# One wait of a load queue is moved from normalised rows to a weight transfer

## The chip, the cores and the metric

The kernel runs on one core of a Trainium2 chip. The core has five engines with a queue of instructions each: TensorE (PE in the profile; its weight loads are listed as PEld), VectorE (DVE), ScalarE (ACT), GpSimd (POOL) and SyncE (SP), which here only issues transfers. Transfers are issued from SP, from POOL and, at the start, from ACT, and all of them are carried by the same 16 DMA engines. The metric is the device time in microseconds of one execution, as a median of several runs.

## The reference

Two blocks follow each other. The first is cosine attention over 8 batches of 12 heads, 448 rows of 64 elements each:

```python
q_n = q / (norm(q) + 1e-6);  k_n = k / (norm(k) + 1e-6)
scores = q_n @ k_n.T / tau            # tau = 0.1
attn = softmax(scores)
attn_out = attn @ v
x = attn_out.transpose(0, 2, 1, 3).reshape(3584, 768)
```

The second is a two-layer product with a leaky ReLU between:

```python
h = x @ w_in                          # 768 -> 2048
g = maximum(0.01 * h, h)
out = g @ w_out                       # 2048 -> 768, float32
```

All inputs are float32. The kernel computes its products in bf16 with float32 sums.

## The kernel before, in words

**Slots.** Queries and keys are handled in 48 slots. In the first two batches (slots 0 to 11, six for each batch) a slot is one pair of heads, with its q and its k. From slot 12 on, two pairs of heads form a unit, and each unit has two slots, or halves: the even slot is the q half, the odd slot the k half. The third batch begins there: slot 12 is the q half of the first unit, slot 13 its k half, slot 14 the q half of the second unit and slot 15 its k half.

**The way of a slot.** `load_qk` (lines 142 to 165) issues its transfers from SP into one of four rotating buffers (`qk_h`); from slot 12 on, these are two transfers of 64 partitions, both on line 150. `squares` multiplies the rows by themselves on POOL (line 216 from slot 12 on, line 224 before). `sums` adds them up on VectorE (line 232; line 238 before slot 12). `roots` takes the norms on ScalarE (lines 245 and 246). `normalise` divides on VectorE (lines 253, 254, and 260 or 270), which writes `qn` and, with the squares, sets the buffer free for the slot four further on. `transposes` then turns the tile: through TensorE (line 284) for early slots, through VectorE (line 306) and six SP transfers per unit (line 315) from slot 12 on.

**What uses it.** `scores` forms the products of q and k on TensorE (line 346) and their exponentials on ScalarE (line 355). `attend` forms the row totals and the products with v on TensorE (line 366), inverts the totals on ScalarE (lines 377 and 378) and scales on VectorE (line 397). The units use lines 417, 423, 442 and 467 or 473 for the same.

**The two-layer product.** `first` (line 494) multiplies with `w_in_sb` and puts the result through the leaky ReLU on ScalarE (line 505); `second` (line 531) multiplies with `w_out_sb`, and VectorE copies the result out of PSUM (line 541) for SP to store (line 548). For the first chunk of rows `second` takes all its tiles against the first half of the output columns, and then all against the second half. `feed_groups` puts such groups into the stream of TensorE between the steps of attention.

**Weights.** `load_w_in` and `load_w_out` issue from POOL and convert from float32 to bf16 on the way. `load_w_out(1)`, the second half of the output columns, is called on line 777, and its last column is the last column of `w_out_sb`. POOL also issues the loads of v (lines 176, 184 and 202).

**Order.** All instructions stand in an order written out by hand; every engine takes its own in that order, and one that waits holds all behind it. Eight PSUM banks are dealt out by `banks` (line 75), which hands out the one used longest ago. Two helpers hold a queue back on purpose:

```python
def hold_loads(s):
    nc.sync.dma_start(out=behind, in_=qn[s][0:1, 6, 0, 0:1])

def hold(x):
    gp.tensor_copy(out=seen, in_=x)
```

`hold_loads(s)` is a transfer of a single element out of the normalised rows of slot s. Its data is not used: SP cannot issue it, nor what stands behind it, before `qn[s]` is written. `hold` does the same to POOL.

In the stretch of the change, s is 6, so that `load_qk(s + 6)` loads slot 12, and so on. The SP queue reads: hold on slot 9, load 12, hold on slot 10, load 13, hold on slot 11, load 14, load 15 (line 832), load 16 (line 842). On POOL, the squares of slots 12 and 13 follow the `hold` of slot 11 (`settle`, line 805), and those of slot 14 follow the `hold` of slot 12. On VectorE, `sums(13)` (line 834) stands ahead of the copies of the output tiles fed after it; on ScalarE, `roots(13)` (line 836) stands ahead of the exponentials of line 838.

Of the kernel before, what the change touches and what calls it, by code (L numbers as in the profile page):

```python
# [16 lines left out]
def kernel(  # L17
# [10 lines left out]
    nc = tc.nc  # L28
    B, H, S, D = q.shape
    N_tok, D_model = out.shape  # L30
# [10 lines left out]
    MT = D_ff // 128  # L41
# [56 lines left out]
    w_out_sb = cpool.tile([128, MT, D_model], BF16, name="w_out_sb")  # L98
# [43 lines left out]
    def load_qk(s):  # L142
        if s >= NSLOT:
            return
        whole = ldp.tile([128, 14 * D], F32, name="qk_h")
        if s >= OLD:
            u, which = divmod(s - OLD, 2)
            for w, pair in enumerate(UNITS[u][1]):
                b, h0 = pair // NPAIR, 2 * (pair % NPAIR)
                nc.sync.dma_start(  # L150
                    out=whole[64 * w : 64 * w + 64],
                    in_=(q, k)[which][b, h0 : h0 + 2].rearrange("h (p t) d -> (h p) (t d)", t=14),
                )
            raw[s] = whole
            return
        b, h0 = s // NPAIR, 2 * (s % NPAIR)
        q_h, k_h = halves(whole)
        nc.sync.dma_start(out=q_h[:, :, 0:3], in_=main(q, b, h0, 2))
        nc.sync.dma_start(out=k_h, in_=main(k, b, h0, 2))
        for i, x in enumerate((q, k)):  # L160
            nc.sync.dma_start(
                out=q_h[64 * i : 64 * i + 64, :, 3],
                in_=x[b, h0 : h0 + 2, MAIN:S].rearrange("h p d -> p h d"),
            )
        raw[s] = (q_h, k_h)
# [5 lines left out]
    def load_v(j):  # L171
        if j >= B * NQ:
            return
        b, jj = divmod(j, NQ)
        vb[j] = vbp.tile([128, 4, 3, D], BF16, name="v_b")
        gp.dma_start(out=vb[j], in_=main(v, b, 4 * jj, 4))
# [405 lines left out]
    behind = cpool.tile([1, 1], BF16, name="behind")  # L582
# [29 lines left out]
    def hold_loads(s):  # L612
        nc.sync.dma_start(out=behind, in_=qn[s][0:1, 6, 0, 0:1])
# [133 lines left out]
    s, j = NPAIR, NQ - 1  # L747
# [46 lines left out]
    hold(qn[s + 4][:, 6, 0, 0:1])  # L794
    squares(s + 5)
    load_v(s // 2 + 2)
    hold_loads(s + 4)
    load_qk(s + 7)
    feed_groups(0, 1)

# [4 lines left out]
    def settle(s, more=()):  # L805
        normalise(s)
        if s >= OLD:
            transposes(s)
        hold(qn[s][:, 6, 0, 0:1])
        for x in (*more, s + 2):  # L810
            squares(x)
# [7 lines left out]

    scores(s + 3, (0, 1, 2))  # L820
    settle(s + 5, (s + 6,))
    hold_loads(s + 5)
    load_qk(s + 8)
    feed_groups(0, 1)
    sums(s + 6)
# [66 lines left out]
    for n, tiles in enumerate(visits):  # L892
        s = preps.get(n, NSLOT)
# [98 lines left out]
```

## Time and profile before

| what | us |
|---|---|
| median of 3 runs (416.55 to 417.8) | 416.8 |
| the profiled execution's own time | 416.43 |
| its span, first to last instruction | 414.6 |
| TensorE busy | 407.1 |
| ScalarE busy | 250.2 |
| VectorE busy | 221.5 |
| POOL busy | 114.6 |
| `w_out_sb`, issue to landing, 2 transfers (least and most) | 21.3, 23.2 |
| `qk_h` from the k input, from slot 12 on, issue to landing (median) | 4.3 |

Times within the span count from its first instruction. An engine is counted as busy only in its own arithmetic; the issue of a transfer is not counted. In the timeline a row gives start, length, engine, line, operation, what is written and read, the number of like instructions merged into the row, and in brackets how long the engine had stood idle and what released it. The queue of transfers issued by POOL is q0, that of those issued by SP and ACT is mainly q1; the DMA view gives packets, MB and the time that the packets took as a share of 16 engines, which can pass 100% since packets overlap.

### The profile page before, as it was taken

What the parts mean: (1) busy time and instruction counts of PE and PEld (TensorE: products, weight loads), DVE (VectorE), ACT (ScalarE), POOL (GpSimd) and SP (SyncE); (2) the same over time, 40 slices, a digit from 0 to 9 for tenths busy, and PEclk for the clock granted to TensorE, in tenths of its full rate; (3) what the DMA queues carried; (4) which work ended last, traced back from release to release, by engine and by line L of the source; (5) the groups of instructions that cost most, each with busy time, mean ns of one, the idle gap of its engine ahead of it and who ended that gap; (6) DMA issues with size and microseconds to landing.
All of it is one profiled execution on the core that took longest, in us unless ns stands there. A gap on an engine that the chain in (4) does not pass through costs nothing.

```text
span 414.6 us, 11342 instructions
## 1 busy us (share of the span) xinstructions
PE 407.1 (98%) x4799; PEld 212.3 (51%) x4799; DVE 221.5 (53%) x387; ACT 250.2 (60%) x431; POOL 114.6 (28%) x149
## 2 busy tenths in 40 slices
PE   8899999999999999999999999999999999999997
PEld 3335555544555555544455555554445555654565
DVE  6977976855778556766474964464621301210022
ACT  5997876378657785668865688547764464004300
POOL 4875543433234132413331433122210000000000
PEclk9999999999999999999999999999999999999999
DMA  7999998775377851884275681742442100020022
GB/s 195 242 214 220 210 234 187 181 223 129 60 206 182 204 132 22 204 229 99 53 186 157 151 229 43 175 126 84 91 90 68 51 39 3 38 77 0 2 76 76
DMA packets 41964, 53.82 MB, mean 130 GB/s; under 512 B 12474, under 2 KB 32314, under 8 KB 41914
## 3 DMA queue, kind: packets, MB, share of 16 engines
q1 hardware_dynamic: 25738, 41.01, 35.0%
q0 software_dynamic: 15488, 11.80, 19.7%
q8 instruction: 37, 0.61, 0.6%
q10 hardware_dynamic: 688, 0.30, 0.2%
q14 instruction: 13, 0.11, 0.1%
HBM read 45.61 MB, written 11.01 MB: 137 GB/s over the span
## 4 chain that ended last, share of the span: by engine, by line
PE 87%; DMA 4%; ACT 3%; DVE 3%; POOL 2%; SPq 1%; issue 1%; POOLq 0%
PE ps L531 34%; PE ps L494 34%; PE ps L442 9%; PE ps L417 7%; ACT pe L355 2%; DMA qk_h<-in_k_dram 2%; PE ps L366 2%; DVE qn L270 1%; DMA xT<-in_k_dram 1%; DMA xT<-in_q_dram 1%; POOL sq L224 1%; PE ps L346 1%; POOL sq L216 1%; DVE ss L238 0%; SPq L131 0%
## 5 line engine op out<-in xcount | busy, mean ns | idle before, releaser
L531 PE MATMUL ps<-w_out_sb,hT 128*128 128x384 bf16 (+1 forms) x912 | 151.3, 324 | 0.3 <-DVE xT L397 0.3
L494 PE MATMUL ps<-xT,w_in_sb 128*128 128x384 bf16 (+1 forms) x768 | 151.1, 353 | 0.0
L423 ACT ACTIVATE pe<-ps 128x896 bf16<-128x896 f32 x126 | 108.9, 915 | 46.1 <-PE ps L417 46.1
L531 PEld LDWEIGHTS <-hT 128*128 128x128 bf16 x912 | 86.5, 98 | 64.3 <-issue 10.0
L494 PEld LDWEIGHTS <-w_in_sb 128*128 128x128 bf16 x768 | 72.6, 98 | 74.3 <-issue 9.7
L505 ACT ACTIVATE hT<-ps 128x384 bf16<-128x384 f32 (+1 forms) x128 | 67.4, 552 | 56.0 <-PE ps L494 55.0
L541 DVE COPY osb<-ps 128x384 f32<-128x384 f32 (+1 forms) x57 | 31.2, 548 | 100.7 <-PE ps L531 100.6
L216 POOL TENSOR_TENSOR sq<-qk_h 128x896 f32<-128x896 f32 x36 | 61.0, 1695 | 9.2 <-DMA qk_h<-in_k_dram 7.7
L616 POOL CAST seen<-qn 128x1 f32<-128x1 bf16 x46 | 8.5, 185 | 169.4 <-DVE qn L260 160.5
L260 DVE TENSOR_TENSOR qn<-qk_h,r 128x896 bf16<-128x896 f32 x36 | 42.4, 1176 | 1.2
L232 DVE TENSOR_REDUCE ss<-sq 128x14 f32<-128x910 f32 x36 | 38.0, 1054 | 1.1 <-POOL sq L216 1.1
L355 ACT ACTIVATE pe<-ps 128x896 bf16<-128x896 f32 x42 | 35.9, 917 | 1.8 <-PE ps L346 1.7
L417 PE MATMUL ps<-qkT 64*32 64x448 bf16 x1008 | 36.5, 353 | 0.0
L253 DVE TENSOR_REDUCE r<-norms 128x14 f32<-128x28 f32 x48 | 8.6, 178 | 48.3 <-ACT norms L246 47.7
L467 DVE TENSOR_TENSOR xT<-ps,rb 128x448 bf16<-128x448 f32 x32 | 18.4, 617 | 23.2 <-PE ps L442 21.5
L306 DVE STREAM_TRANSPOSE tt<-qn 128x448 f32<-128x448 f32 x36 | 29.6, 821 | 0.9
L442 PE MATMUL ps<-pe,vq 64*32 64x448 bf16 x1008 | 27.0, 349 | 0.0
L245 ACT ACTIVATE ss<-ss 128x14 f32<-128x14 f32 x48 | 10.3, 214 | 25.4 <-DVE ss L232 24.4
L417 PEld LDWEIGHTS <-qkT 64*32 64x32 bf16 x1008 | 13.1, 91 | 19.2 <-issue 14.5
L442 PEld LDWEIGHTS <-vq 64*32 64x32 bf16 x1008 | 14.5, 92 | 8.0 <-issue 0.3
L442 PE MATMUL ps<-pe,ones 64*32 64x448 bf16 x560 | 15.1, 349 | 0.0
L346 PE MATMUL ps<-qkT 64*64 64x448 bf16 (+1 forms) x132 | 12.9, 359 | 2.1 <-ACT pe L355 1.2
(53 smaller groups left out, 218.9 us busy)
## 6 DMA issues: line engine op xcount, KB each, us to landing
qk_h<-in_q_dram SPq DMA_DIRECT2D x36, 224.0 KB, 4.0
qk_h<-in_k_dram SPq DMA_DIRECT2D x36, 224.0 KB, 4.3
out_dram<-osb SPq DMA_DIRECT2D x20, 384.0 KB, 2.3
qkT<-tt SPq DMA_DIRECT2D x72, 56.0 KB, 3.3
qkT<-tt SPq DMA_DIRECT2D x36, 112.0 KB, 3.5
vq<-in_v_dram POOLq DMA_DIRECT2D x16, 224.0 KB, 5.0
w_in_sb<-in_moe_w_in_dram POOLq DMA_DIRECT2D x4, 768.0 KB, 11.2
w_out_sb<-in_moe_w_out_dram POOLq DMA_DIRECT2D x2, 1536.0 KB, 22.3
```

The source lines that it names most:

```text
L216: gp.tensor_tensor(sq[:, :, :D], x, x, op=ALU.mult)
L232: nc.vector.tensor_reduce(ss[s], sqs[s], axis=AX.X, op=ALU.add)
L260: nc.vector.tensor_tensor(qn[s].rearrange("p m d e -> p m e d"), raw[s].rearrange(f"p ({t[1:-1]} d) -> p m e d", e=n, d=D), r.rearrange(f" ...
L306: nc.vector.transpose(out=to.rearrange(("p g (c m) -> p m g c", "p g (m c) -> p m g c")[which], m=7), in_=qn[s].bitcast(F32).rearrange("p ...
L355: nc.scalar.activation(out=dst, in_=sc[:, :, :S], func=AF.Exp, scale=inv_tau)
L417: nc.tensor.matmul(out=sc[32 * strip : 32 * strip + 32, a, :S], lhsT=x[rows, c0 : c0 + 32], rhs=x[rows, 0:S], start=True, stop=True,)
L423: nc.scalar.activation(out=pq[u, i], in_=sc[:, :, :S], func=AF.Exp, scale=inv_tau)
L442: nc.tensor.matmul(out=po[32 * strip : 32 * strip + 32, w, :S], lhsT=weights, rhs=pq[us[x if two else 0], i][rows, a, :], start=(i == 0), ...
L494: nc.tensor.matmul(out=pm[:, :n], lhsT=w_in_sb[:, kt, m * 128 : (m + 1) * 128], rhs=xT[c // 2][:, kt, c0 : c0 + n], start=(done + i == 0), ...
L505: nc.scalar.activation(out=hT[c][:, m, :n], in_=pm[:, :n], func=AF.Prelu, alpha=0.01)
L531: nc.tensor.matmul(out=po2[:, : hi - lo], lhsT=hT[c][:, m, ts * 128 : (ts + 1) * 128], rhs=w_out_sb[:, m, half * HALF + lo : half * HALF + ...
L541: nc.vector.tensor_copy(out=o[:, cols], in_=po2[:, : hi - lo])
```

## The change

The one-element transfer ahead of load 13 reads the last element of `w_out_sb` in place of an element of `qn[10]`, so that SP waits there until `load_w_out(1)` has landed. The one-element transfer ahead of load 14 is removed. Loads 13, 14 and 15 stand behind the new wait. Everything else keeps its order.

```diff
@@ -794,7 +794,7 @@
     hold(qn[s + 4][:, 6, 0, 0:1])
     squares(s + 5)
     load_v(s // 2 + 2)
-    hold_loads(s + 4)
+    nc.sync.dma_start(out=behind, in_=w_out_sb[0:1, MT - 1, D_model - 1 :])
     load_qk(s + 7)
     feed_groups(0, 1)
 
@@ -819,7 +819,6 @@
 
     scores(s + 3, (0, 1, 2))
     settle(s + 5, (s + 6,))
-    hold_loads(s + 5)
     load_qk(s + 8)
     feed_groups(0, 1)
     sums(s + 6)
```

## The prediction

> **What bounds the kernel now.** I read the first part of the page, then the list of waits of TensorE, then the chain of work between 40 and 95 us, and last the timeline and the DMA view of the stretch that the change touches. The page:
>
> ```profile
> PE 407.1 (98%) x4799; PEld 212.3 (51%) x4799; DVE 221.5 (53%) x387; ACT 250.2 (60%) x431; POOL 114.6 (28%) x149
> ```
>
> TensorE is busy for 98%, and from 60 us to the end its list of waits holds one entry of 0.3 us, at 70.49 us. So the order of work on TensorE after 60 us is a block without holes: whatever stops it there for a microsecond adds about a microsecond. The chain of work (start, length, what) says what TensorE leans on shortly before 70 us:
>
> ```profile
> 54.85 7.55 DMA qk_h<-in_k_dram
> ...
> 64.72 1.11 DVE ss L232
> ```
>
> This is load 13 (the k half of the first unit): it landed at 62.40, was squared on GpSimd (POOL) and summed on VectorE, and its root was taken on ScalarE at 65.86. The chain runs through this load already, so a later landing meets almost no reserve. Timeline, with idle time and releaser in brackets:
>
> ```profile
> 49.12 1.16 POOL L110 DMA_DIRECT2D w_out_sb<-in_moe_w_out_dram  x1
> ...
> 53.64 0.60 SPq L613 DMA_DIRECT2D behind<-qn  x1
> ...
> 54.33 1.11 SPq L150 DMA_DIRECT2D qk_h<-in_k_dram  x2
> ...
> 62.53 2.16 POOL L216 TENSOR_TENSOR sq<-qk_h 128x896 f32<-128x896 f32 x1 [3.64 <-DMA qk_h<-in_k_dram]
> ...
> 64.72 1.10 DVE L232 TENSOR_REDUCE ss<-sq 128x14 f32<-128x910 f32 x1 [0.51 <-POOL sq L216]
> ...
> 65.74 0.55 DVE L541 COPY osb<-ps 128x384 f32<-128x384 f32 x1
> ...
> 67.27 0.75 PE L366 MATMUL ps<-pe,ones 128*32 128x448 bf16 x12
> ...
> 70.49 4.99 PEld L531 LDWEIGHTS <-hT 128*128 128x128 bf16 x32 [0.69 <-DMA w_out_sb<-in_moe_w_out_dram]
> ```
>
> POOL stood 3.64 us for load 13. The second half of the output weights left at 49.12, took 21.3 us (the landing time of its tile's view), so it landed at 70.4, and TensorE's weight load stood for it until 70.49. Last, how fast the POOL queue (q0), on which these weights travel, moves when the other queue is quiet, from 56 to 58 us:
>
> ```profile
> q0 software_dynamic: 540, 0.41, 132.0%
> q1 hardware_dynamic: 4, 0.00, 0.3%
> ```
>
> 0.41 MB in 2 us, 0.205 MB/us, the weights' own pace.
>
> **The change part by part.** Edit 1: the one-element transfer in front of load 13 waits for the second half of the output weights instead of for the norms of slot 10. Before, SP was released at 53.6; now at T, when the weights land. The instruction list of the changed kernel has the semaphore of that POOL transfer at this place, where VectorE's stood. Edit 2: the transfer in front of load 14 goes. Load 14 then follows load 13 at once.
>
> T, step by step. The weights are 1536 KB, 98 kB for each of 16 engines; 0.205 MB/us over 16 is 12.8 kB/us, so 7.7 us. They queue behind a v load issued at 48.31 whose landing took 8.5 us: the slowest engine gets to the weights at 56.8. 56.8 + 7.7 = 64.5. A second way: from 58 to 71 us queue q1 held 49.7% of the engines, 6.5 us, most of it loads 13 to 16, which now wait; 70.4 - 6.5 = 63.9. Lower bound: all engines finish together; from 58 us on q0 moved 1.10 MB, of which 0.2 MB is the next v load, and 0.90 MB at 0.205 is 4.4 us: 62.4. Upper bound: nothing is gained from the quiet, 70.4. I take 64.5, since the landing is that of the slowest engine.
>
> From T to load 13's landing: the release at 53.64 and the start of its second half at 54.85 are 1.21 us apart; then the landing. In the stretch of 72 to 100 us, without weights under way, loads on this line took 3.4, 4.1 and 5.8 us (least, median, most). I take 4.1: T + 5.3, 69.8 instead of 62.4.
>
> Who stands behind it. POOL squares slot 13 (1.68 us, the median of its group), with slot 14 queued after it. VectorE's sum of slot 13 starts 0.14 + 1.70 after the landing, 71.6, and queued behind it on VectorE stands the copy at 65.74 that empties a PSUM bank; it ends 1.57 us after the sum's start, at 73.2. The next instruction of TensorE that needs this bank is the row of totals at 67.27 (by the rotation of the banks in the code: the bank of the second half-0 output tile is the next single one to be dealt). So TensorE stops at 67.3 and goes on at landing + 3.46 = T + 8.8 = 73.3: 6.0 us later. ScalarE's root of slot 13 (65.86) starts at 72.8, +6.9, and the three exponentials queued behind it too; TensorE needs the first at 68.04 + 6.0 and has it (67.07 + 6.9 = 74.0): no more added.
>
> What it gives back: the wait for the weights at 70.49 goes. TensorE itself stood 0.26 us: -0.26.
>
> What is late next: the turned tile of unit 0 (VectorE 72.57, then six transfers on SP from 73.37 to 77.14, landing 3.3 us later, 80.4) is needed by TensorE at 80.9. With +6.9 it lands at 87.3; TensorE would be there at 86.6, so up to 0.7 us more if nothing else slows TensorE.
>
> TensorE after a stop. Before shows no stop of over 1 us but the one at the start: after 1.65 us of idleness the 512-column products followed each other every 0.425 us for 5.1 us, and from 6.75 us on every 0.21:
>
> ```profile
> 5.89 0.15 PEld L605 LDWEIGHTS <-pe 128*128 128x128 bf16 x1 [0.28 <-issue]
> 6.32 0.15 PEld L605 LDWEIGHTS <-pe 128*128 128x128 bf16 x1 [0.28 <-issue]
> 6.75 1.44 PEld L605 LDWEIGHTS <-pe 128*128 128x128 bf16 x7 [0.28 <-issue]
> ```
>
> 12 products at 0.21 us too much are 2.5 us. After a stop of 6 us this can come back: 0 (it belongs to the start alone) to 2.5. I take 2.5, as the nearest row is that of a TensorE that has stood; it also covers the 0.7 us above. Beside it stands the Trainium skill, "TensorE: Matmul & The Clock Gate", Part 1: the array falls to half its clock after an idle window of about 3.4 us, and climbs back after a busy one. By that rule a 6.0 us stop is long enough and the sum is the one below; without it, it would be rival A's. No run here shows a stop of this length in the middle of the kernel.
>
> Costed at nothing: the transfer that is gone (0.6 us of SP, which stands from 64.4 to 73.4 anyway), and with it the completion semaphores of later transfers move by one, all of long-landed ones. Loads 14, 15 and 16 leave at T + 1.9 to T + 5.6 and land by 76 at the latest; their squares stood at 66.26, 72.81 and 76.67 and come at 71.6 (right behind slot 13's), 79.7 and 83.6: POOL's queue covers 15 and 16, and load 14, landed by about 72, is followed by a sum that comes only at 80. If that cover went, the sum of slot 14 would be next.
>
> Sum: 6.0 - 0.26 + 2.5 = +8.2 us. The profiled execution took 416.43 us: 424.6. It stands 0.37 us under the median of 416.8, inside the spread of the three runs.
>
> **The rivals.**
> A. The same stop without the slow restart: 6.0 - 0.26 + 0.7 = +6.4, 422.9. For it: no slow stretch after the start in before; against it: no stop in before to try it.
> B. The weights land at the lower bound, 62.4, and load 13 in 3.4 us: the stop is 62.4 + 1.21 + 3.4 + 3.46 - 67.27 = 3.2, so +2.9, 419.4; with the restart 421.9. For it: an emptier DMA. Against it: the slowest engine starts on the weights at 56.8.
> C. The weights gain little: T near 70.4. The stop is 70.4 + 8.8 - 67.3 = 11.9, and +14.1 with the restart, 430.6. For it: first to last engine now spread over some 7 us. Against it: 6.5 us of q1 traffic really goes.
> D. Not slower. The hold opens so early that load 13 lands no later than TensorE can bear. Its stop is T - 58.5; it vanishes for T up to 58.5, and then only the 0.26 us is gained: 416.2, no measurable change. For it: loads took up to 7.5 us while the weights were under way, and 4.1 after, so the later start buys 3.4 us. Against it: 1.57 MB in 9.4 us after issue, behind a v load that itself lands at 56.8; q0 never kept over 0.205 MB/us in the stretches I read. By the fit in the Trainium skill, "DMA: Bandwidth & Descriptors", Anatomy of one DMA (2.0 us + bytes / 436 GB/s), 1.57 MB would take an estimated 5.6 us and land at 54.7, so D would hold and the time be D's 416.2. The trace disagrees: 21.3 us for this transfer, and 11.2 us (median) for one of half its size.
>
> **How the numbers follow.** Chances: forecast (T of 63.5 to 66.5 with a restart cost) 0.50; A 0.17; B 0.12; C 0.14; D 0.07. The range leaves out the upper half of C, the lowest of B and D: 419.5 to 429.5. About 0.3% (1.25 us) is what a measurement of this kernel can tell from no change. A, B, C and the forecast are slower by more than that: 0.93. D is 'same' but for unknown gains from the emptier DMA: same 0.05, faster 0.02.
>
> **What would show it.** In the changed profile: the one-element transfer and load 13 leave SP near 64 to 65 us; POOL's squares on line 216 wait some 11 us for that load; VectorE's sum on line 232 starts near 71.6; TensorE has a hole of about 6 us before the totals on line 366, released by VectorE's copy; the weights' wait on line 531 is gone; products after the hole are spaced at twice their time for some microseconds, or the granted clock dips. It is wrong if the weights land before 60 us, if the hole is absent, or if TensorE finds other work in it (its order is fixed, so I see none).

## The result, and the profile after

The changed kernel took 424.02 us (median of 6 runs, 422.52 to 424.49) against 417.02 us of the kernel before (6 runs). The ratio is 1.0163, with a 95% interval of 1.0144 to 1.0181: 7.0 us slower. The forecast was 424.6, between 419.5 and 429.5, and slower. The profiled execution took 424.18 us, 7.75 more than that of before. Every ratio below is to runs of the kernel before that were made along with it.

The list of waits of TensorE from 50 us to the end (who waits and for whom; us in total, times, longest), in the changed kernel:

```profile
PE ps L366 <- DVE osb L541: 5.9, 1, 5.9
PE ps L494 <- issue: 0.2, 1, 0.2
```

Before, the same list had one entry (what it waited for is settled below, with the third experiment):

```profile
PE ps L531 <- DVE xT L397: 0.3, 1, 0.3
```

Now there is one stop of 5.9 us, at the totals on line 366, and it is VectorE's copy out of PSUM that ends it. The wait on line 531 is gone. The chain of work says what the copy was late for (start, length, what):

```profile
49.43 15.24 DMA w_out_sb<-in_moe_w_out_dram
...
64.70 0.60 SPq L797
...
65.91 4.28 DMA qk_h<-in_k_dram
...
70.33 1.69 POOL sq L216
...
72.04 1.10 DVE ss L232
73.14 0.48 DVE osb L541
73.62 0.04 issue
73.66 4.09 PE ps L366 x36
```

The chain goes back from TensorE over the copy, the sum, the squares and load 13 to the transfer of the output weights, which ends at 64.68. In the timeline of before, SP had been let go for load 13 at 53.64. Before, queue q1, on which the loads of q and k travel, had moved 0.45 MB between 58 and 61 us. Now, between 57 and 61 us, the DMA view shows no traffic of q1, and of the POOL queue q0 this (packets, MB, share of 16 engines):

```profile
q0 software_dynamic: 1051, 0.81, 130.6%
```

0.81 MB in 4 us is the 0.20 MB/us of before: the quiet lets the weights keep their own pace, and no more. They land after 15.2 us instead of 21.3. The timeline around the stop, with idle time and releaser in brackets:

```profile
65.02 2.77 PE L531 MATMUL ps<-w_out_sb,hT 128*128 128x384 bf16 x16
...
70.32 1.68 POOL L216 TENSOR_TENSOR sq<-qk_h 128x896 f32<-128x896 f32 x1 [10.98 <-DMA qk_h<-in_k_dram]
...
72.04 1.10 DVE L232 TENSOR_REDUCE ss<-sq 128x14 f32<-128x910 f32 x1 [7.38 <-POOL sq L216]
...
73.17 0.22 ACT L245 ACTIVATE ss<-ss 128x14 f32<-128x14 f32 x1 [9.28 <-DVE ss L232]
...
73.66 1.31 PE L366 MATMUL ps<-pe,ones 128*32 128x448 bf16 x12 [5.87 <-DVE osb L541]
```

POOL stands for 10.98 us, VectorE for 7.38, ScalarE for 9.28, and TensorE, the only one whose time counts, for 5.87. The 12 products of the totals then take 1.31 us; before, they took 0.75. Busy time by stretch (TensorE, its weight loads, VectorE, ScalarE, POOL, then granted clock, DMA share and GB/s) says why:

```profile
69.00:70.00 1.00, 0.00 (x0) 0.00 (x0) 0.00 (x0) 0.00 (x0) 0.00 (x0) 1.00 0.96 251
70.00:71.00 1.00, 0.00 (x0) 0.00 (x0) 0.00 (x0) 0.00 (x0) 0.68 (x1) 0.59 1.01 244
...
76.00:77.00 1.00, 1.00 (x19) 0.43 (x15) 0.00 (x0) 0.97 (x3) 0.00 (x0) 0.50 0.00 0
77.00:78.00 1.00, 1.00 (x24) 0.37 (x16) 0.83 (x2) 0.10 (x1) 0.00 (x0) 0.99 0.00 0
```

The granted clock falls to 0.50 near 70.2 (0.59 over that microsecond is 0.18 us of full clock), during the stop, and is back at 77.0. TensorE worked for 3.35 us of that time, from 73.66 on, at half rate.

The account: from the start of the totals to the first product against the second half of the weights, TensorE took 3.22 us before (67.27 to 70.49), of which it stood 0.26. After, it took 4.52 (73.66 to 78.18). So the restart, the loss by the half rate after the stop, cost 4.52 - 2.96 = 1.56 us. The totals would have followed the row of line 531 at 65.02 without a gap, near 67.72 (2.70 later, as 64.57 and 67.27 stood before): they came 5.94 late. 5.94 + 1.56 - 0.26 = 7.24. The row on line 531 moved by 7.69, of which 0.44 was there already at the products on line 346 (60.48 before, 60.92 after), ahead of the stop and not explained here. The span grew by 7.8.

### The profile page after: what moved, and what is told of

Its sections match the earlier page's. It is cut to its first block, busy times and chain, and to the rows that moved or that the text cites. A ratio compares the mean times of both kernels' runs of the same rounds, so it can differ in the third digit from the quotient of the medians.

```text
span 422.4 us, 11322 instructions
## 1 busy us (share of the span) xinstructions
PE 406.8 (96%) x4783; PEld 212.7 (50%) x4799; DVE 220.8 (52%) x387; ACT 250.6 (59%) x431; POOL 114.6 (27%) x149
## 4 chain that ended last, share of the span: by engine, by line
PE 83%; DMA 8%; DVE 3%; POOL 2%; ACT 2%; issue 1%; SPq 1%; POOLq 0%
PE ps L531 33%; PE ps L494 31%; PE ps L442 9%; PE ps L417 7%; DMA w_out_sb<-in_moe_w_out_dram 4%; DMA qk_h<-in_k_dram 3%; PE ps L366 2%; DVE qn L270 1%; POOL sq L224 1%; DVE ss L238 1%; ACT pe L355 1%; DMA xT<-in_q_dram 1%; POOL sq L216 0%; PE ps L346 0%; POOL v_rem L184 0%
## 5 line engine op out<-in xcount | busy, mean ns | idle before, releaser
L216 POOL TENSOR_TENSOR sq<-qk_h 128x896 f32<-128x896 f32 x36 | 60.5, 1681 | 15.2 <-DMA qk_h<-in_k_dram 15.1
L442 PE MATMUL ps<-pe,ones 64*32 64x448 bf16 x560 | 15.1, 349 | 0.0
```

Of the source, the lines that this page charges most:

```text
L216: gp.tensor_tensor(sq[:, :, :D], x, x, op=ALU.mult)
L442: nc.tensor.matmul(out=po[32 * strip : 32 * strip + 32, w, :S], lhsT=weights, rhs=pq[us[x if two else 0], i][rows, a, :], start=(i == 0), ...
```

## The experiments

Theory M: the cost is the late landing of load 13, passed on through POOL, VectorE and one PSUM bank to TensorE, and a slow restart. Its rivals were that the bunch of loads 14 to 16 costs (R), that waiting on the weights' tile costs by itself (W), that every microsecond of delay costs its share (L), and that the slow rows after the stop have nothing to do with the stop (C).

**The second edit alone.** Against the kernel before:

```diff
-    hold_loads(s + 5)
```

> Only the second edit: the hold ahead of load 14 is gone, the hold ahead of load 13 still waits for the norms of slot 10. Theory M (the cost is load 13's late landing, handed on through POOL, VectorE and one PSUM bank to TensorE): load 13 leaves SP at 54.3 as before; load 14 now leaves right behind it, some 3 us earlier, and may make load 13 and the weights land up to 1 us later: 416.8 to 418.2. Rival R (loads 14 to 16 crowding is what costs): 420 or more.

Measured: 416.88 us (10 runs), a ratio to the kernel before of 0.9987 (0.9975 to 0.9998), so 0.1% faster at most, near the edge of what can be told. Load 14 left SP at 55.97 instead of 58.97, and POOL took up the squares of slot 13 at 63.25 (62.53 before). R is wrong as far as this edit goes. In its profile the weights landed after 22.0 us instead of 21.3, and TensorE stood 0.87 us for them instead of 0.26; the median shows nothing of it.

**The first edit alone.** Against the kernel before:

```diff
-    hold_loads(s + 4)
+    nc.sync.dma_start(out=behind, in_=w_out_sb[0:1, MT - 1, D_model - 1 :])
```

> Only the first edit: load 13 waits for the weights, and the hold on slot 11 stays ahead of load 14. Slot 11 is normalised at 57 us, long before SP gets there, so the kept transfer costs SP only some 0.7 us. Theory M: as the changed kernel, 423.3 to 424.8, TensorE stopped about 5.9 us before the totals. Rival R (both edits are needed, since loads 14 to 16 in a bunch cost): clearly less, 418 to 421.

Measured: 423.71 us (4 runs), ratio 1.0154 (1.0134 to 1.0174), not apart from the changed kernel's 1.0163. Its waits of TensorE from 50 us on:

```profile
PE ps L366 <- DVE osb L541: 5.9, 1, 5.9
```

The same stop at the same place. The whole loss is in the first edit. The restart is not the same, though: from the start of the totals at 72.99 to the first product against the second half of the weights at 78.23 TensorE took 5.24 us, so that by the account above the restart cost 2.28 us here, against 1.56. The granted clock fell at 71.08 and was back at 77.91, so that TensorE worked for 4.92 us at half rate instead of 3.35.

**The same wait, one load later.** Against the kernel before:

```diff
-    hold_loads(s + 5)
+    nc.sync.dma_start(out=behind, in_=w_out_sb[0:1, MT - 1, D_model - 1 :])
```

> The wait for the weights stands one load later: load 13 keeps its hold on slot 10, load 14 waits for the weights in place of slot 11, and 15 and 16 stand behind it. Theory M: load 13 lands near 62 as before; the weights land near 66 to 67, load 14 near 72, just about when its squares are due (sum of slot 14 stood at 73.1): 416.6 to 418.0. Rival R (the bunch behind the weights is what costs, whichever load leads it): 421 to 424.

Measured: 417.21 us (10 runs), ratio 0.9993 (0.9978 to 1.0009): no difference. SP in its timeline:

```profile
53.95 1.11 SPq L150 DMA_DIRECT2D qk_h<-in_k_dram  x2
66.66 0.60 SPq L822 DMA_DIRECT2D behind<-w_out_sb  x1
67.35 1.11 SPq L150 DMA_DIRECT2D qk_h<-in_q_dram  x2
```

Load 13 leaves at 53.95 as in the kernel before, and loads 14 to 16 stand behind the weights until 66.66, later even than in the changed kernel. That costs nothing: TensorE has no stop at the totals, its wait for the weights is gone, and the sum of slot 14 comes at 74.0 (73.1 before), from which a wait of 0.6 us on line 417 remains. (The profile of before names VectorE's line 397 for the wait on line 531. Here that row begins at 70.10, while the first scaling on line 397 runs from 69.74 to 70.37, and it does not wait; so before it was the weights that it waited for.) So neither the bunch (R) nor the wait on this tile (W) is the price. It is which load stands first behind it.

**A wait on the same tile that ends early.** Against the changed kernel:

```diff
-    nc.sync.dma_start(out=behind, in_=w_out_sb[0:1, MT - 1, D_model - 1 :])
+    nc.sync.dma_start(out=behind, in_=w_out_sb[0:1, MT - 1, 0:1])
```

> The changed kernel with the waiting transfer reading an element of the first half of the weights, which landed at 52.3 in the profile of before, so the wait ends no later than the old one at 53.6. Theory M: load 13 leaves at 54 as before, 416.8 to 418.2, like the kernel that only drops the second hold. Rival W (waiting on the weights' tile costs by itself, by its semaphore or by what the queue does behind it): 421 to 424.

Measured: 417.14 us (10 runs), ratio 1.0001 (0.9987 to 1.0015). The waiting transfer left SP at 52.83 and load 13 at 53.52. Only the moment of the release matters; W is out.

**A smaller dose.** Against the changed kernel, the wait is on the v load that was issued just ahead of the weights:

```diff
-    nc.sync.dma_start(out=behind, in_=w_out_sb[0:1, MT - 1, D_model - 1 :])
+    nc.sync.dma_start(out=behind, in_=vb[s // 2 + 1][0:1, 3, 2, D - 1 :])
```

> A smaller dose: the changed kernel with the waiting transfer reading the last element of the v load issued at 48.3, which landed at 56.8, so the release comes some 3 us later than before instead of 11. Theory M (the stop is the landing of load 13 minus 63.8, and nothing before that): load 13 leaves at 57.5 and lands between 62.1 (4.1 us) and 65.6 (7.5 us, as the weights are still under way), so a stop of 0 to 1.8 us, too short for a slow restart: 416.8 to 418.8, with about 418 if the landing is slow. Rival L (each us of delay costs its share, no reserve): 3 of 11 us, so 419.

Measured: 419.07 us (6 runs), ratio 1.0039 (1.0027 to 1.0052), by the ratio 1.6 us slower than the kernel before: just above the range of M, on the number of L. The median alone does not tell them apart; the profile does. Load 13 in its chain of work:

```profile
57.26 0.60 SPq L797
...
58.47 6.70 DMA qk_h<-in_k_dram
```

and its waits of TensorE from 50 us on, with the row on line 417 from its timeline below them:

```profile
PE ps L366 <- DVE osb L541: 1.1, 1, 1.1
PE ps L417 <- DVE xT L397: 0.5, 2, 0.3
```

```profile
82.00 0.57 PE L417 MATMUL ps<-qkT 64*32 64x448 bf16 x16
82.87 0.35 PE L417 MATMUL ps<-qkT 64*32 64x448 bf16 x1 [0.30 <-DVE xT L397]
```

With the weights still under way the load needs 6.70 us and lands at 65.2. This profile runs 0.2 us late (60.69 at the products on line 346, 60.48 before), so the formula of the prediction gives 65.2 - 0.2 - 63.8 = 1.2 us, and the stop is 1.1. Load 13 lands 2.6 us later than before and the stop is 1.1, so some 1.5 us were reserve: L, which has none, is out. The rest is a second wait, 0.5 us, on line 417, which the expectation had left out. It is not for the turned tile of unit 0, which the prediction named as late next: the first 16 products of the row read that tile and do not wait. The next one writes to a bank that VectorE's scaling on line 397 still has to empty (82.19 to 82.82), and it starts 0.05 us after that, at 82.87. The scaling comes late because the sums and roots ahead of it in the queues of VectorE and ScalarE do. The clock stays at 1.00. 1.1 + 0.5 - 0.26 = 1.3 us, of the 1.6 measured.

**TensorE kept busy, first try.** Against the changed kernel, ahead of the totals:

```diff
+    for i in range(60):
+        nc.tensor.matmul(
+            out=ps[:, 0, S:512], lhsT=id128, rhs=id128[:, : 512 - S],
+            start=(i == 0), stop=(i == 59),
+        )
     attend(NQ + 1)
```

> The changed kernel with 60 small products of constants (128x128 weights, 64 columns) given to TensorE just before the totals, where it stands still; their output goes to unused columns of PSUM. Theory M: the stop stays, as its cause is elsewhere, the clock stays at 1.0, and the slow restart (about 1.7 us in the profile of the changed kernel) goes: 422.0 to 422.9, against 424.0. Rival C (the rows after the stop are slow for another reason, such as PSUM or the operands just written): 423.7 to 424.5. If the small products take longer than the stop, some tenths are added.

Measured: 428.42 us (5 runs), ratio 1.0257 (1.0234 to 1.0279). It does not test what it was for. The small products wrote to columns that nothing uses, but in a bank whose exponential was still to come, and its wait came with it:

```profile
74.93 3.15 PE L841 MATMUL ps<-id 128*128 128x64 bf16 x60 [8.02 <-ACT pe L355]
78.01 0.75 PE L366 MATMUL ps<-pe,ones 128*32 128x448 bf16 x12
```

The stop became longer, 8.0 us, and the products came after it. It shows that this bank was not free; whether another was is not shown. The granted clock fell here too, at 70.87, and was back at 77.70. The small products filled the rest of the slow time, and the totals behind them took 0.75 us again, after a stop of 8.0 us, which fits the clock as the cause of the slow rows.

**TensorE kept busy, in its own bank.** Against the changed kernel, the output tile just ahead of the stop is computed three times over, the last time for use:

```diff
-            for m in range(MT):
+            for m in (3 if (c, ts, half) == (0, 2, 0) else 1) * list(range(MT)):
```

> The changed kernel, in which the output tile of TensorE just ahead of the stop (16 products, 2.7 us) is computed three times over into its own bank, the last time for use: 32 products more, some 5.2 us, inside the 5.9 us in which TensorE stood. In the try before, the small products had stood behind the exponentials and so not filled the stop. Theory M (the stop costs 5.9 us and the halved clock after it 1.7): the totals start when they did, the clock stays at 1.0, 422.0 to 422.9 (424.0 less 1.7 and what the shorter second window takes). Rival C (the slow rows after the stop come from something else than the stop): 423.7 to 424.5, clock still 0.99.

Measured: 422.99 us (4 runs), ratio 1.0141 (1.0128 to 1.0155), between the two ranges and next to that of M. Its timeline and its stretches:

```profile
64.60 7.97 PE L531 MATMUL ps<-w_out_sb,hT 128*128 128x384 bf16 x48
72.51 0.75 PE L366 MATMUL ps<-pe,ones 128*32 128x448 bf16 x12
```

```profile
70.00:72.00 2.00, 2.00 (x14) 1.22 (x13) 1.11 (x2) 0.00 (x0) 0.98 (x2) 1.00 1.03 249
72.00:74.00 2.00, 2.00 (x36) 1.03 (x38) 1.01 (x2) 1.94 (x5) 1.58 (x1) 1.00 0.76 181
```

5.2 us of added work fill the stop, the granted clock stays at 1.00, and the totals take 0.75 us again instead of 1.31. C is out: it is the stop that makes the rows after it slow. The mean granted clock of all four timed runs is 0.999 or 1.000, and that of the six runs of the changed kernel 0.991 to 0.995. The gain against the changed kernel is 1.0 us by the medians, less than the 1.56 us of the restart; TensorE now waits 0.5 us on line 417, for the scaling on line 397 as in the smaller dose. The intervals of the two ratios overlap (1.0128 to 1.0155, 1.0144 to 1.0181), so the time alone does not show the gain; the clock and the rows do.

**Not from the change: the weights issued first.** Against the kernel before, from which the hold ahead of load 14 is taken out too (not shown in the lines below):

```diff
-    load_v(s // 2 + 1)
     load_w_out(1)
+    load_v(s // 2 + 1)
```

> Not from the change: the kernel before without the hold ahead of load 14, and the second half of the output weights issued from POOL ahead of the v load of line 176 instead of behind it. The weights then start on the engines one v load (0.2 MB, about 1 us) earlier and should land near 70, about when TensorE wants them (70.2); its wait for them (0.9 us in the kernel without the hold) shrinks: 416.2 to 417.0 against 417.0 to 417.4 for the kernel before. Rival: the v load, now last, is late for the products on line 366 at 67.9, and takes back as much or more: 417 to 418.

Measured: 421.23 us (6 runs), ratio 1.0079 (1.0059 to 1.0100): a clear miss. What the rival named came about, the late v load, but at more than its price of 417 to 418. The v load behind 1.5 MB of weights on the same queue landed after 22.0 us:

```profile
71.45 0.75 PE L366 MATMUL ps<-pe,v_b 128*32 128x448 bf16 x12 [3.39 <-DMA v_b<-in_v_dram]
```

TensorE stood for 3.39 us, and in the profiled run that was enough for the clock:

```profile
72.00:73.00 1.00, 1.00 (x23) 0.49 (x16) 0.49 (x1) 0.00 (x0) 0.00 (x0) 0.73 0.07 17
...
75.00:76.00 1.00, 1.00 (x6) 0.47 (x4) 0.96 (x2) 0.98 (x2) 0.00 (x0) 0.56 0.00 0
```

Not in every run: in two of the six the mean granted clock was 1.000, and they took 419.07 and 419.52 us; in the other four it was 0.992 to 0.996, and they took 421.16 to 421.85.

## Why the prediction was right

| step | forecast | measured |
|---|---|---|
| weights land, SP is let go (T) | 64.5 | 64.68 |
| second half of load 13 leaves, after T | 1.21 | 1.23 |
| its landing time | 4.1 | 4.28 |
| POOL's wait for it | 11 | 10.98 |
| sum of slot 13 begins | 71.6 | 72.04 |
| TensorE's stop | 6.0 | 5.9 |
| wait for the weights, gone | -0.26 | gone |
| slow restart | +2.5 | +1.56 |
| sum, profile against profile | +8.2 | +7.24, and 0.44 from ahead of the stretch |

The forecast, 424.6, is nearer to the measured 424.02 than its terms are to theirs: the restart was put 0.94 us too high, and 0.44 us that nobody forecast came in ahead of the stretch. The two moments in the table, T and the sum of slot 13, carry such a late start as well: the weights were issued at 49.43 instead of 49.12. That part of the agreement is luck; the path and the stop are not.

**T.** The longer of the two ways was right. From issue to landing the weights took 15.1 to 15.8 us in the four profiles in which load 13 stands behind them; the two ways gave 15.4 and 14.8. That fits the reason given, that the landing is that of the slowest engine, which first has to finish the v load ahead. That load landed after 8.6 us here (8.5 before), and the weights then kept 0.20 MB/us. That the stretch before the change showed this pace at all, in the 2 us in which the other queue was quiet, is what made T a sum of rows.

**The way of the delay.** Squares, sum, copy, bank, totals: all in the order forecast, each released by the one before it. The first edit alone brings the whole loss, the second none, and the same wait one load later costs nothing. A release that comes 3 us late instead of 11 gives the stop of the formula (1.1 us for 1.2), so the reserve in the formula, from 62.4 to 63.8, is also right. The prediction's sentence that a later landing meets "almost no reserve" does not fit its own formula: it is 1.4 us. Not run was the copy put ahead of the sum on VectorE, which would try that link alone; it rests on the rows of the profiles.

**The restart.** Here the size was off. The step took the 2.5 us of the start of the kernel, where TensorE worked at half rate for 5.1 us. In the middle of the kernel the half rate lasted longer, 6.8 us (70.2 to 77.0), but it began during the stop, and TensorE worked for only 3.35 us of it: 1.56 us lost. With the first edit alone it worked for 4.92 us of it and lost 2.28, close to the 2.5, behind a stop of the same 5.9 us. The term that holds is the working time inside the slow stretch, times a little under a half. That the start of the kernel was slow for the same reason, the clock, was a reading from the spacing of its products; it holds, as the trace of before records the rise of the clock at 6.84 us, where the spacing halves. (The windows view prints 1.00 ahead of that first record.) The Trainium skill, "TensorE: Matmul & The Clock Gate", Part 1, has the clock fall after an idle window of about 3.4 us and rise after a busy one. The lengths agree: the stretch of 6.8 us is two such windows and that of 3.4 us in the last experiment is one. The fall does not agree to the letter: in the changed kernel it came 2.4 us after the stop began, so the window that ended there had work in it. Rival A, no restart cost, is out by the profile.

**What is late next.** This step did not come about as it was told. In the changed kernel there is no wait on line 417. Where there is one, 0.5 or 0.6 us in three of the experiments, the scaling on line 397 ends it, and in none of TensorE's lists does a wait stand for the turned tile of unit 0. The forecast put the step under cover of the restart, so nothing of the sum hangs on it.

**The rivals B, C and D.** B needed all engines to finish the weights together, and C no gain from the quiet: T at 64.68 is neither. D needed T below 58.5. Its page, the Trainium skill's "DMA: Bandwidth & Descriptors", Anatomy of one DMA, with its estimated 5.6 us for these 1.57 MB, does not describe this transfer: even with the other queue quiet from 56 us on it took 15.2 us, of which some 8 passed until the v load ahead had landed (57.2) and 7.4, still more than the estimate, at 0.2 MB/us.

What stays open: why q0 alone does not pass 0.2 MB/us here. Its transfers read float32 and write bf16, so they read twice what the view counts; no run varied that.

## What to carry to other kernels

When a queue is held back on purpose, price the hold by the first transfer behind it: follow that one to the engine that is the bound, and compare its new landing with the moment at which the bound needs it. The same hold cost 7 us in front of load 13 and nothing in front of load 14. And where the bound is TensorE, a stop of some 3 us or more can bring slow rows behind it: here they added 1.56 and 2.28 us to stops of 5.9, and to one of 3.4 us, by the mean clocks, something in four runs of six and nothing in two.

## What the runs showed of the hardware that was not expected

The granted clock changes only on a beat of its own, and a stop meets that beat where it happens to. Four traces have a slow stretch (us from the start of the span, by the trace's record of the granted clock):

| run | first rise | TensorE stops | fall | TensorE goes on | rise |
|---|---|---|---|---|---|
| changed kernel | 5.33 | 67.79 | 70.19 | 73.66 | 77.01 |
| first edit alone | 6.23 | 67.10 | 71.08 | 72.99 | 77.91 |
| kept busy, first try | 6.02 | 66.91 | 70.87 | 74.93 | 77.70 |
| weights issued first | 7.61 | 68.06 | 72.47 | 71.45 | 75.88 |

From the first rise to the fall it is 64.85 us in all four, and from the fall to the rise 6.83 us in three and 3.41 in the last. These are 19, 2 and 1 times 3.413 us. The fall comes 2.4 to 4.4 us after the stop begins; in the last row it comes a microsecond after TensorE has gone on. In the changed kernel TensorE had worked for 1.0 us of the beat that ended in the fall, and in the last row too, so a beat need not be idle throughout. How much work in a beat keeps the clock up was not measured.

So the cost of a stop depends on how it meets the beat. Half the rate for one beat takes 3.41 x 0.5 / 420 = 0.004 off the mean granted clock of a run. The six timed runs of the changed kernel fall into 0.991 or 0.992 in three (424.18 to 424.49 us) and 0.995 in the other three (422.52 to 423.86). That these are runs with two slow beats and with one is argued from the means, and not shown by a trace.
